# A block-recurrent cross-attention with a three-way maxout FFN: a head in a new order, with the second slice of batch 0 ahead of the third slice of G

## The chip, the core and the metric

The kernel runs on one core of a Trainium2 chip. The metric is device time in microseconds, lower is better; the time of a kernel is the median of several runs. A core has a matrix engine (TensorE, PE in the profile, which also shows its weight loads as PEld), a vector engine (VectorE, DVE), a scalar engine (ScalarE, ACT), a general engine (GpSimd, POOL) and a sync engine (SyncE, SP). DMA is issued from the queues of SP, ACT and POOL. PE writes only into PSUM, and ACT and DVE carry results out of it.

## The reference

Sizes: batch B = 8, heads H = 8, sequence S = 512, states Ns = 32 for each head, width D = 64; d_model = 512, d_ff = 768. Inputs and output are float32.

```python
scores  = x @ state^T / sqrt(64);  a  = softmax(scores, over states)
xread   = a @ state
scores2 = state @ x^T / sqrt(64);  a2 = softmax(scores2, over tokens)
sread   = a2 @ x
y   = concat([xread, sread], axis=2)          # rows of a batch: 512 tokens, then 32 states
y   = y.transpose(0, 2, 1, 3).reshape(8 * 544, 512)
h   = maximum(maximum(y @ w1, y @ w2), y @ w3)
out = h @ w_out
```

## The kernel before

Per batch the kernel never forms `xread`. It builds G = (block-diagonal states) @ W for the three matrices at once (`g_slice` and `g_run`, L363 of `g_mm`), so that the first layer is `pw = G^T aT`, with `aT` the transposed attention weights. One slice of the first layer is 128 of the 768 columns of d_ff for one batch: `layer1(b, m)` issues 6 matmuls into three PSUM banks, one for each matrix (L416). Three instructions make the maximum of the three: ACT copies the first bank to SBUF (`max_first`, L431), and DVE takes the maximum with the second bank (`max_second`, L436) and with the third (`max_third`, L440), which writes `ht`. The second layer is `layer2(b, j)`: 6 matmuls into one bank (L447), which ACT or DVE copies out (L454).

Ahead of that, for each batch: `x` is loaded and transposed (`xT`; by PE for batches 0 and 1, by a transposing DMA on SP's queue for the others), the scores are 16 small matmuls (L262), ACT exponentiates them (L269), DVE sums and inverts (L276, L278), POOL (or DVE) multiplies (L284), and the weights are transposed to `aT` (by PE at L295 for batches 0 and 1, by DMA afterwards). The states' own read is `sread` (L327).

The states come in four loads of two batches each, `load_st(k, q)` for batches 2k and 2k+1 on queue q (L152, tiles `stf0` to `stf3`). `states_cast` casts them (L217), `states_turn` transposes them on PE (L222, tile `pt`) and `states_place` copies them into the block-diagonal tile `bd` (L228). Everything of batches 2 and 3 that uses `bd` stands behind the load of `stf1`.

W1, W2 and W3 arrive in pieces by `load_w(m0, m1, i)`: columns 128*m0 to 128*m1 of matrix i (0, 1, 2) on POOL's queue (L179). G's slice m of batches 0 and 1 needs these columns of all three matrices.

The order is written out by hand: strings of short words (`FIRST`, `EACH` once for each batch, `LAST`) are walked by `perform`, and each word calls one function, whose instructions go to their engines in that order. So every engine runs its own instructions in the order of the words, and waits where a semaphore says so. The words that matter here: `lst` load states, `stc`/`stt`/`stp` cast, turn and place them, `lw` load a piece of W, `lxg` load half of a batch of x (four of its eight heads), `g`/`gc` a slice of G and its copies out, `l1` a slice of layer 1, `m0`/`ma`/`mb` its three maximum instructions, `l2`/`l2c` layer 2 and its copy, `busy` one filler matmul of 512 columns on a zero tile (`keep_busy`, L211), whose result nobody reads. A letter behind a word names the engine or queue (A for ACT, D for DVE, P for POOL, S for SP). `BANKS` gives the PSUM bank of each one-bank tile in order of use (four banks), `PAIRS` that of each two-bank tile. The words of one batch in `EACH` make PE run, for batch b and the one before it: 24 + 6 + 6 layer-1 matmuls, 24 layer-2 matmuls, the scores, G and `sread`.

Behind all this stands a branch that redoes the softmax with a maximum subtracted if a sum left a safe range; it is not taken with these inputs.

Of the kernel before, what the change touches and what calls it, by code (L numbers as in the profile page):

```python
# [17 lines left out]
FIRST = """  # L18
    lst 0 A; lxu 0 0 S; zero; clr 0; clr 1; clr 2; clr 3; warm; lxg 0 1; busy 1; xones 1; ident; busy 1;
    lxg 1 0; busy 1; busy 1; stc 0 D; busy 1; busy 1; busy 1; busy 1; busy 1; lxg 1 1; stt 0; busy 2;  # L20
    cxu 0 0 D; xt 0 0; stp 0 A; busy 1; xt 0 1; busy 1; xtc 0 0 D; lw 0 2 1; lw 0 2 2; xtc 0 1 D;
    busy 1; sc 0 0; busy 1; lw 0 1 0; busy 1; sc 0 1; lw 1 3 0; ex 0 0; busy 1; busy 1; xt 1 0; sum 0 0;
    lw 2 3 1; busy 1; ex 0 1; sum 0 1; xt 1 1; busy 1; xtc 1 0 AD; busy 1; lw 2 3 2; busy 1; xtc 1 1 A;
    busy 1; wt 0 0 P; wt 0 1 P; xones 0; sc 1 0; ex 1 0; busy 1; sc 1 1; at 0 0; atc 0 0 A; sr 0;
    busy 1; sum 1 0; lw 3 4 0; at 0 1; lst 1 A; lw 3 6 2; lw 3 6 1; ex 1 1; wt 1 0 D; g 0 0; gc 0 0 D;
    busy 1; sum 1 1; g 1 0; sr 1; atc 0 1 A; lw 4 6 0; wt 1 1 P; at 1 0; srs 0; g 1 1; g 0 1; stc 1 P;
    l1 0 0; gc 1 1 D; gc 1 0 A; g 1 2; g 0 2; atc 1 0 A; busy 1; gc 0 1 A; m0 0 0; at 1 1; lxg 2 1;
    srs 1; ma 0 0; l1 0 1; lxg 2 0; gc 0 2 A; l1 0 2; atc 1 1 D; l1 1 0; m0 0 1; m0 0 2; lwo; m0 1 0;
    gc 1 2 A; mb 0 0; xtd 2; l1 1 1; g 0 3; m0 1 1; lst 3 S; lst 2 A; ma 0 1; gc 0 3 A; g 1 3; pad 2;
    stt 1; gc 1 3 A; mb 0 1; ma 0 2; mb 0 2; ma 1 0; mb 1 0; l1 1 2; ma 1 1; g 0 5; m0 1 2; ones; g 0 4;  # L30
    mb 1 1; stp 1 DA; l1 0 3; gc 0 4 A; ma 1 2; g 1 4; gr 2 1792 2304; gc 0 5 D; m0 0 3; mb 1 2; l1 1 3;
    l1 0 5; gc 1 4 A; gr 2 0 512; g 1 5; m0 1 3; ma 0 3; mb 0 3; ma 1 3; l1 1 4; grc 2 1792 2304 A;
    mb 1 3; m0 0 5; gr 2 1280 1792; stc 2 P; lxg 3 1; gr 2 512 1024; ma 0 5; l1 0 4; stt 2; sc 2 -;
    gc 1 5 A; m0 1 4; grc 2 0 512 D; mb 0 5; lxg 3 0; ma 1 4; grc 2 1280 1792 AD; m0 0 4; ma 0 4;
    mb 0 4; mb 1 4; xtd 3; l2 0 3; l2 0 1; ex 2 -; l1 1 5; stp 2 A; l2c 0 3 D; stc 3 P; l2 0 2; sum 2 -;
    l2c 0 1 D; stt 3; l2 0 0; m0 1 5; ma 1 5; l2c 0 2 A; grc 2 512 1024 D; wt 2 - P; sr 2; mb 1 5;
    srs 2; gr 2 1024 1280; l2c 0 0 D; so 0 0 2 P; lx 4; so 0 2 4 P; stp 3 A; grc 2 1024 1280 A; atd 2;
"""
EACH = """
    pad 1; gr 1 1792 2304; gr 1 0 512; grc 1 1792 2304 AD; l2 -1 0; l2 -1 1; l1 0 0; grc 1 0 512 D;  # L40
    l2c -1 0 A; m0 0 0; sc 1 -; l2 -1 3; gr 1 1024 1280; ex 1 -; xtd 2; gr 1 1280 1792; l2c -1 1 D;
    ma 0 0; gr 1 512 1024; mb 0 0; sr 1; grc 1 1024 1280 A; l1 0 1; l1 0 2; sum 1 -; l1 0 3; srs 1;
    l1 0 5; l2c -1 3 A; m0 0 1; m0 0 2; ma 0 1; mb 0 1; ma 0 2; m0 0 3; mb 0 2; srt -2; ma 0 3;
    wt 1 - P; m0 0 5; mb 0 3; l2 -1 2; grc 1 1280 1792 A; grc 1 512 1024 A; ma 0 5; mb 0 5; l2c -1 2 D;
    l1 0 4; so -1 2 4 P; m0 0 4; ma 0 4; lx 3; mb 0 4; atd 1; ap -2 A; so -1 0 2 P;
"""
LAST = """
    srt 6; l1 7 0; srt 7; l2 6 0; l1 7 2; m0 7 0; l1 7 3; l1 7 4; ap 7 D; m0 7 2; srt 5; ap 6 A; ma 7 0;
    m0 7 3; mb 7 0; ap 5 A; l2c 6 0 D; ma 7 2; l2 6 1; l1s 0; l2 6 2; m0 7 4; mb 7 2; l1 7 1; l2c 6 1 A;
    ma 7 3; m0 s 0; l2c 6 2 A; l1s 2; l1 7 5; ma 7 4; mb 7 4; look; ma s 0; m0 7 1; m0 s 2; mb s 0;  # L50
    so 6 2 3 S; m0 7 5; mb 7 3; l1s 1; ma 7 1; mb 7 1; ma s 2; mb s 2; ma 7 5; m0 s 1; ma s 1; l1s 5;
    so 6 0 1 S; mb 7 5; l2p 7 2 384 512; l1s 3; m0 s 5; ma s 5; mb s 1; m0 s 3; mb s 5;
    l2pc 7 2 384 512 A; l2p 7 0 384 512; l2p 7 3 256 512; sop 7 2 384 512 P; ma s 3; l2p 7 2 128 384;
    mb s 3; l2p 7 0 0 128; l2pc 7 0 0 128 A; l2pc 7 3 256 512 D; l2p 7 1 0 128; l2p 7 3 0 256;
    l2pc 7 0 384 512 D; flag; l2pc 7 1 0 128 A; l2pc 7 2 128 384 A; l1s 4; m0 s 4; l2 6 3;
    sop 7 0 0 128 P; ma s 4; sop 7 0 384 512 P; mb s 4; l2p s 0 256 512; so 6 1 2 P; l2 s 1;
    sop 7 3 256 512 A; l2c 6 3 D; l2p 7 2 0 128; sop 7 1 0 128 S; l2p s 0 0 256; so 6 3 4 A;
    l2pc 7 3 0 256 D; l2pc s 0 256 512 D; sop s 0 256 512 A; l2pc 7 2 0 128 A; l2p 7 1 128 384;
    sop 7 2 0 128 A; l2p 7 0 256 384; l2p 7 1 384 512; l2pc s 0 0 256 A; l2p 7 0 128 256;
    l2pc 7 1 128 384 A; l2c s 1 D; sop 7 3 0 256 S; sop 7 2 128 384 P; l2pc 7 0 256 384 D;  # L60
    sop 7 1 128 384 A; l2pc 7 1 384 512 D; sop 7 1 384 512 A; l2pc 7 0 128 256 D; sop 7 0 128 256 A;
    sos 1 S; sop s 0 0 256 S; sop 7 0 256 384 S; hold; vl;
"""

BANKS = """
# [3 lines left out]
"""  # L69
PAIRS = """  # L70
    0101100101 1010010010 1010101010 1010101010 10
# [4 lines left out]
def kernel(  # L76
# [21 lines left out]
    J = 4  # L98
# [19 lines left out]
    st = [data.tile([128, 4, 2, D], BF16, name=f"st{k}") for k in range(B // 2)]  # L118
# [15 lines left out]
    xT, e, a, aT, G, ht, osb, xp = {}, {}, {}, {}, {}, {}, {}, {}  # L134
    open_ps = {}

    def new(d, b, shape, name, bufs=2):
        d[b] = work.tile(shape, BF16, tag=name, bufs=bufs, name=name)


    homes = {n: iter("".join(t.split())) for n, t in (("b", BANKS), ("w", PAIRS))}
# [28 lines left out]
    def load_x_uncast(b, g, q):  # L170
        o = work.tile([128, J, d_model], F32, tag="osb", bufs=3, name="osb")
        x_f[b, g] = o.rearrange("p j f -> p (j f)")[:, 0:HS * J * D].rearrange("p (s jd) -> p s jd", s=HS)
        queue[q].dma_start(out=x_f[b, g], in_=x_heads(b, g))
# [42 lines left out]
    def states_cast(k, c):  # L216
        copier[c](out=st[k], in_=st_f[k].unsqueeze(2).to_broadcast((128, 4, 2, D)))  # L217

    def states_turn(k):
        p = open_ps["st", k] = bank([128, 4, 128], BF16, "pt")  # L220
        for t in range(4):
            nc.tensor.transpose(p[:, t, :], st[k][:, t].rearrange("p c d -> p (c d)"), ident)  # L222

# [7 lines left out]
    def x_turn(b, g):  # L231
        if g == 0:
            new(xT, b, [128, H, 2, 128], "xT", bufs=3)
# [7 lines left out]
    def x_turned(b, g, c):  # L241
        p, w = open_ps.pop(("x", b, g)), HS // len(c)
# [4 lines left out]
    def x_turn_dma(b):  # L247
        new(xT, b, [128, H, 2, 128], "xT", bufs=3)
        nc.sync.dma_start_transpose(out=xT[b].rearrange("p h j t -> p (h j) t"), in_=x_sb[b][:, 0:XW])

# [3 lines left out]
    def scores(b, g=None):  # L254
        if not g:
            new(e, b, [128, J, 2, HS, Ns], "e")
# [11 lines left out]
    def exps(b, g=None):  # L268
        nc.scalar.activation(out=parity(e[b], g), in_=open_ps.pop(("s", b, g)), func=AF.Exp, scale=scale)  # L269
# [10 lines left out]
    def weights(b, g, c):  # L280
        if not g:
            new(a, b, [128, J, 2, HS, Ns], "a")
# [7 lines left out]
    def a_turn(b, g):  # L290
        if g == 0:
            new(aT, b, [128, J, 2, 128], "aT", bufs=3)
# [4 lines left out]
    def a_turned(b, g, c):  # L297
        copier[c](out=aT[b][:, :, g, :], in_=open_ps.pop(("a", b, g)))

    def a_turn_dma(b):  # L300
        new(aT, b, [128, J, 2, 128], "aT", bufs=3)
# [4 lines left out]
    def pad(b):  # L306
        xp[b] = work.tile([128, HS, J, 2 * D + 2], BF16, tag="xp", name="xp")
# [7 lines left out]
    def sread(b):  # L315
        w = D + 1 if b in xp else 2 * D
        p = open_ps["r", b] = bank([128, 2, w], F32, "psr")
        for j in range(J):
            for g in range(2):
                for s in range(HS):  # L320
                    if b in xp:
                        both = xp[b][:, s, j, g * D:g * D + D + 1]
                    else:
# [4 lines left out]
                        p[32 * s:32 * s + 32, g], e[b][:, j, g, s, :], both,  # L328
# [38 lines left out]
    def new_g(b):  # L367
        if b not in G:
            new(G, b, [128, 2, 3, d_ff], "G", bufs=3)


    def g_slice(b, m):
        new_g(b)
# [4 lines left out]
    def g_sliced(b, m, c):  # L378
        p = open_ps.pop(("g", b, m))
# [5 lines left out]
    def g_run(b, c0, c1):  # L385
        new_g(b)
        n = c1 - c0
        if n > 256:
# [9 lines left out]
    def g_ran(b, c0, c1, c):  # L398
        p, ps = open_ps.pop(("g", b, c0))
# [10 lines left out]
    def maxout(b, m, n, lhs, rhs, nk, by_k=False):  # L410
        if m == 0 and b not in ht:
# [132 lines left out]
    def perform(plan, base=0):  # L544
        for op in plan.replace("\n", " ").split(";"):
# [5 lines left out]
            if batches and args[0] != "s":  # L551
                args[0] += base
                if args[0] >= B:
                    continue
# [123 lines left out]
```

## Time and profile before

| | us |
|---|---|
| median of 3 runs | 153.05 |
| lowest and highest | 152.54, 153.25 |
| span of the profiled execution, first to last instruction | 151.4 |
| the median less that span | 1.6 |
| PE, DVE, ACT, POOL busy | 146.4, 118.9, 82.8, 57.0 |

The time of the profiled execution itself is not given apart from its span; what lies around the span is taken as 1.6 us, from the median of the runs. In the profile a line such as L416 is a line of the kernel before; `out<-in` names tiles with buffer numbers left out; times count from the first instruction. The granted TensorE clock of this execution is 1.000 in the view by cores.

### The profile page before, as it was taken

Reading aid. Unit: us, or ns where it says so; the run is one execution under the profiler, and the core shown is the slowest. Engines: PE = TensorE matmul, PEld = TensorE weight load, DVE = VectorE, ACT = ScalarE, POOL = GpSimd, SP = SyncE. Lnnn points to the kernel's source line nnn. Section 1 sums busy time; section 2 is a strip of 40 time slices with the busy share of each in tenths; the row PEclk is TensorE's granted clock in tenths of the full one; section 3 lists DMA queues with packets and bytes.
Section 4 is the critical chain, followed back from the end, with each engine's and each line's share of the span. In section 5 each row is a group of like instructions: output and inputs, shape, how many; then the busy total and the mean of one; then the engine's idle time right before and its main releaser. Section 6 shows DMA issues by size and latency. Waiting matters only on the chain.

```text
span 151.4 us, 3635 instructions
## 1 busy us (share of the span) xinstructions
PE 146.4 (97%) x1431; PEld 73.8 (49%) x1431; DVE 118.9 (79%) x204; ACT 82.8 (55%) x143; POOL 57.0 (38%) x79
## 2 busy tenths in 40 slices
PE   6999799999999999999999999999999999999992
PEld 2566343335445443544354435443544446679771
DVE  6477698999977898879987988798879887675353
ACT  3368558976364665466646664666466653331220
POOL 6979650561528505540554046414331200001500
PEclk9999999999999999999999999999999999999999
DMA  3999999979737979999589749974503250300455
GB/s 115 211 189 195 207 198 195 151 149 139 139 74 167 230 59 265 129 223 132 155 124 230 144 130 140 232 122 141 218 0 78 68 226 4 122 18 17 175 180 196
DMA packets 39108, 22.29 MB, mean 147 GB/s; under 512 B 23072, under 2 KB 36896, under 8 KB 39088
## 3 DMA queue, kind: packets, MB, share of 16 engines
q0 software_dynamic: 15872, 13.96, 48.7%
q1 hardware_dynamic: 21776, 6.82, 23.4%
q10 hardware_dynamic: 1440, 1.25, 2.7%
q8 instruction: 12, 0.20, 0.5%
q14 instruction: 8, 0.07, 0.2%
HBM read 15.20 MB, written 8.91 MB: 159 GB/s over the span
## 4 chain that ended last, share of the span: by engine, by line
PE 86%; DMA 6%; POOL 4%; issue 1%; DVE 1%; POOLq 0%
PE pw L416 46%; PE po L447 25%; DMA w<-in_moe_w_dram 6%; PE pg L363 5%; PE po L462 4%; POOL w L179 2%; PE ps L262 2%; PE psr L327 2%; POOL x L168 1%; PE pgh L363 1%; PE pt L222 1%; DVE held L522 0%; PE idle L520 0%; PE idle L211 0%; DVE osb L466 0%
## 5 line engine op out<-in xcount | busy, mean ns | idle before, releaser
L416 PE MATMUL pw<-aT,G 128*128 128x512 bf16 x288 | 66.8, 379 | 0.0
L431 ACT CAST t<-pw 128x512 bf16<-128x512 f32 (+1 forms) x54 | 30.4, 564 | 28.9 <-PE pw L416 27.2
L416 PEld LDWEIGHTS <-G 128*128 128x128 bf16 x288 | 27.2, 98 | 33.2 <-issue 1.9
L436 DVE TENSOR_TENSOR t<-t,pw 128x512 bf16<-128x512 bf16 (+1 forms) x54 | 35.4, 655 | 9.5 <-ACT t L431 7.4
L447 PE MATMUL po<-wout,ht 128*128 128x512 bf16 x168 | 39.9, 379 | 0.0
L440 DVE TENSOR_TENSOR ht<-t,pw 128x512 bf16<-128x512 bf16 x48 | 32.9, 687 | 4.3
L447 PEld LDWEIGHTS <-ht 128*128 128x128 bf16 x168 | 15.3, 98 | 19.0 <-issue 1.7
L284 POOL TENSOR_TENSOR a<-e,rden 128x1024 bf16<-128x1024 bf16 (+1 forms) x9 | 14.5, 1620 | 24.1 <-ACT osb L454 11.1
L477 POOL DMA_DIRECT2D out_dram<-osb x13 | 7.4, 572 | 30.5 <-ACT t L431 27.5
L403 ACT CAST G<-pg 128x1024 bf16<-128x1024 f32 (+1 forms) x17 | 14.3, 875 | 1.3 <-PE pg L363 1.3
L311 POOL COPY xp<-x 128x1024 bf16<-128x1024 bf16 x12 | 12.3, 1062 | 5.5 <-DMA x<-in_x_dram 5.5
L454 DVE COPY osb<-po 128x512 f32<-128x512 f32 x16 | 10.9, 684 | 2.4 <-PE po L447 2.3
L276 DVE TENSOR_REDUCE seen<-e 128x32 f32<-128x1024 bf16 (+1 forms) x10 | 10.0, 999 | 3.6 <-ACT e L269 3.6
L403 DVE CAST G<-pg 128x1024 bf16<-128x1024 f32 (+1 forms) x13 | 12.2, 972 | 0.7 <-ACT G L403 0.7
L454 ACT COPY osb<-po 128x512 f32<-128x512 f32 x13 | 7.7, 593 | 8.9 <-PE po L447 8.9
L269 ACT ACTIVATE e<-ps 128x1024 bf16<-128x1024 f32 (+1 forms) x10 | 8.5, 854 | 6.6 <-PE ps L262 6.4
L363 PE MATMUL pg<-w,bd 64*32 64x512 bf16 (+1 forms) x288 | 10.8, 362 | 0.9 <-DMA w<-in_moe_w_dram 0.9
L211 PE MATMUL idle<-zero 128*128 128x512 bf16 x27 | 10.0, 477 | 1.3 <-DVE zero L187 1.3
L472 POOL DMA_DIRECT2D out_dram<-osb x4 | 2.2, 544 | 19.4 <-ACT osb L466 19.4
L381 ACT CAST G<-pg 128x768 bf16<-128x768 f32 x9 | 7.1, 801 | 3.3 <-PE pg L363 3.1
L416 PE MATMUL pw<-atp,w 128*128 128x256 bf16 x72 | 8.7, 272 | 0.0
L416 PEld LDWEIGHTS <-w 128*128 128x128 bf16 x72 | 6.9, 98 | 1.5
(70 smaller groups left out, 116.0 us busy)
## 6 DMA issues: line engine op xcount, KB each, us to landing
out_dram<-osb POOLq DMA_DIRECT2D x12, 512.0 KB, 3.5
x<-in_x_dram POOLq DMA_DIRECT2D x4, 512.0 KB, 7.3
x<-in_x_dram POOLq DMA_DIRECT2D x7, 256.0 KB, 5.5
w<-in_moe_w_dram POOLq DMA_DIRECT2D x4, 256.0 KB, 7.5
w<-in_moe_w_dram POOLq DMA_DIRECT2D x2, 384.0 KB, 7.9
wout<-in_moe_w_out_dram POOLq DMA_DIRECT2D x1, 768.0 KB, 11.6
out_dram<-osb SPq DMA_DIRECT2D x3, 256.0 KB, 2.4
osb<-in_x_dram SPq DMA_DIRECT2D x1, 512.0 KB, 4.0
```

The source lines that it names most:

```text
L211: nc.tensor.matmul(p, zero[:, 0:128], zero, start=True, stop=True)
L276: nc.vector.reduce_sum(out=den, in_=parity(e[b], g), axis=AX.X)
L284: times[c](out=parity(a[b], g).rearrange("p j g s n -> p j (g s) n"), in0=parity(e[b], g).rearrange("p j g s n -> p j (g s) n"), in1=rdens ...
L311: nc.gpsimd.tensor_copy(out=xp[b][:, :, :, g * (D + 1):g * (D + 1) + D], in_=v[:, g])
L363: nc.tensor.matmul(p(s, g), bd(b, 2 * s + g)[64 * g:64 * g + 64, g, :], f(w_sb[64 * g:64 * g + 64, s]), start=True, stop=True, tile_positi ...
L403: copier[c[g]](out=v[:, g:h], in_=p[:, g:h, 0:c1 - c0])
L416: nc.tensor.matmul(pw[i][:, 0:n], lhs(i, k), rhs(k), start=(k == 0), stop=(k == nk - 1))
L431: nc.scalar.copy(out=t0s[b, m][:, 0:n], in_=open_ps["l", b, m][0][:, 0:n])
L436: nc.vector.tensor_max(t1s[b, m][:, 0:n], t0s.pop((b, m))[:, 0:n], open_ps["l", b, m][1][:, 0:n])
L440: nc.vector.tensor_max(ht[b][:, m, :], t1s.pop((b, m))[:, 0:n], open_ps.pop(("l", b, m))[2][:, 0:n])
L447: nc.tensor.matmul(p, ht[b][:, m, j * 128:(j + 1) * 128], wout_sb[:, m, :], start=(m == 0), stop=(m == NM - 1))
L454: copier[c[i]](out=o[:, j, i * w:i * w + w], in_=p[:, i * w:i * w + w])
```

## The change

The three strings become one flat string, `PLAN`, in which the head (everything up to the first steps of batch 3) stands in another order; from batch 4 on the blocks name, on PE, the same steps in the same order as before, written out for each batch, and the end of the program has the same steps on PE. `BANKS` and `PAIRS` are written anew to fit. A table `PLACES` names the buffer of each work tile, where before a pool rotated two, three or four of them; the buffer is taken when the tile is first written instead of when it is first mentioned. The cast states (`st`) lie in two buffers instead of four. The program before has 27 filler matmuls ahead of the last one that closes the program; the changed one has 17.

```diff
-FIRST = """
-    lst 0 A; lxu 0 0 S; zero; clr 0; clr 1; clr 2; clr 3; warm; lxg 0 1; busy 1; xones 1; ident; busy 1;
...
-    l1 0 0; gc 1 1 D; gc 1 0 A; g 1 2; g 0 2; atc 1 0 A; busy 1; gc 0 1 A; m0 0 0; at 1 1; lxg 2 1;
...
+PLAN = """
+    lst 0 A; lxu 0 0 S; lxg 0 1; zero; ident; lxg 1 0; xones 0; xones 1; lxg 1 1; lw 0 1 0; lw 0 2 2; lw 0 2 1;
...
+    sr 1; atc 0 1 A; at 1 0; g 0 1; gc 1 0 A; atc 1 0 A; srs 1; gc 0 1 D; g 1 1; l1 0 0; m0 0 0; ma 0 0;
+    gc 1 1 AD; lst 1 A; wt 1 1 P; lw 3 6 2; at 1 1; atc 1 1 A; l1 0 1; m0 0 1; mb 0 0; ma 0 1; mb 0 1; g 0 2;
...
 BANKS = """
-    0123012301 2302013012 0130120203 2012313031 3210130213 2012302130 1231021301 2310210230 1320312312
+    0332000013 2131011300 2310132011 2031023021 3201230123 0213021032 0130213021 3012310201 0213201203 1201321031
...
+    def turned(j):
+        return j % 2 * 2 + j // 2
...
     def exps(b, g=None):
-        nc.scalar.activation(out=parity(e[b], g), in_=open_ps.pop(("s", b, g)), func=AF.Exp, scale=scale)
+        new(e, b, [128, J, 2, HS, Ns], "e")
+        nc.scalar.activation(
+            out=parity(e[b], g).rearrange("p (c i) g s n -> p i c (g s n)", i=2),
+            in_=open_ps.pop(("s", b, g)).rearrange("p (i c) g s n -> p i c (g s n)", i=2),
+            func=AF.Exp, scale=scale)
...
+    def tokens(b, j):
+        k = j if b == "s" else turned(j)
+        return slice(k * 128, k * 128 + 128)
+
     def layer2(b, j):
...
-            nc.tensor.matmul(p, ht[b][:, m, j * 128:(j + 1) * 128], wout_sb[:, m, :],
+            nc.tensor.matmul(p, ht[b][:, m, tokens(b, j)], wout_sb[:, m, :],
```

The four token blocks of a batch now lie in another order in `e`, `a` and `aT` (0, 2, 1, 3): ACT writes the exponentials that way in one instruction of as many elements, and `sread` and layer 2 pick the blocks accordingly. Functions for a transposed score path are added and not called.

Three places of the new order, for the engines on which they lie. The first is ACT at the first slices of layer 1. `G_334` and `G_350` are G of batches 0 and 1 before (`G_326` and `G_388` now), `pg` is the PSUM tile of one of their slices, `aT_396` (`aT_390`) is `aT` of batch 1, `t0` is the copy of the first bank of a layer-1 slice, `stf1` the states of batches 2 and 3. Before:

```order
L381 CAST G_350<-pg_351 128x6x128
L298 COPY aT_396<-pat_397 128x4x128
L381 CAST G_334<-pg_414 128x6x128
L431 CAST t0_458<-pw0_425 128x512
L381 CAST G_334<-pg_445 128x6x128
L431 CAST t0_502<-pw0_471 128x512
L431 CAST t0_504<-pw0_482 128x512
```

and now:

```order
L444 CAST G_388<-pg_331 128x6x128
L362 COPY aT_390<-pat_374 128x4x128
L492 CAST t0_414<-pw0_405 128x512
L444 CAST G_388<-pg_396 128x3x128
L190 DMA stf1_75<-in_state_dram 128x256
L362 COPY aT_390<-pat_423 128x4x128
L492 CAST t0_438<-pw0_429 128x512
L444 CAST G_326<-pg_445 128x6x128
```

Between the copies of the first and the second layer-1 slice of batch 0 (`t0_458` and `t0_502`, now `t0_414` and `t0_438`) stood the copy of G's third slice of batch 0 (`G_334<-pg_445`); it now stands behind both (`G_326<-pg_445`). ACT's copy of G's second slice of batch 0 (`G_334<-pg_414`) is gone from it (DVE does it), half of that of batch 1 has come, the second half of `aT` of batch 1 too, and the load of `stf1`, which stood six rows above `t0_458`, follows the first slice now.

The second place is POOL's queue of loads, from the second matrix pieces on. Here `w` pieces of 128 columns have the size 128x4x128, `a` is the product at L284, and `x2` is batch 2. Before:

```order
L179 DMA w_94<-in_moe_w3_dram 128x4x128
L284 TENSOR_TENSOR a_251<-e_180,rden_221 128x4x128
L284 TENSOR_TENSOR a_251<-e_180,rden_228 128x4x128
L198 MEMSET x0_86 128x64
L179 DMA w_94<-in_moe_w1_dram 128x4x128
L179 DMA w_94<-in_moe_w3_dram 128x4x384
L179 DMA w_94<-in_moe_w2_dram 128x4x384
L179 DMA w_94<-in_moe_w1_dram 128x4x256
L284 TENSOR_TENSOR a_332<-e_255,rden_348 128x4x128
L217 CAST st1_79<-stf1_75 128x512
L168 DMA x2_88<-in_x_dram 128x4x256 x2
```

and now:

```order
L217 DMA w_90<-in_moe_w2_dram 128x4x128
L217 DMA w_90<-in_moe_w2_dram 128x4x384
L349 TENSOR_TENSOR a_233<-e_194,rden_200 128x4x128
L349 TENSOR_TENSOR a_233<-e_194,rden_226 128x4x128
L217 DMA w_90<-in_moe_w1_dram 128x4x128
L349 TENSOR_TENSOR a_324<-e_260,rden_266 128x4x128
L349 TENSOR_TENSOR a_324<-e_260,rden_322 128x4x128
L217 DMA w_90<-in_moe_w3_dram 128x4x384
L206 DMA x2_84<-in_x_dram 128x4x256
L217 DMA w_90<-in_moe_w1_dram 128x4x256
L206 DMA x2_84<-in_x_dram 128x4x256
```

One 384-column piece of W is issued ahead of the products of batch 0, both products of batch 1 are POOL's (DVE did one), one half of `x2` goes ahead of the last piece of W (256 columns of W1), and the cast of `stf1`, which stood ahead of both halves, is behind these rows. Higher up in the same queue the first piece of W1 is issued ahead of those of W2 and W3 instead of behind them.

The third place is SP's queue at its start. `osb` is the first half of batch 0's x, loaded as float32 into an output buffer, and `stf3` holds the states of batches 6 and 7. Before:

```order
L173 DMA osb_105<-in_x_dram 128x4x256
L249 DMA_TRANSPOSE xT_511<-x2_88 128x16x128
L152 DMA stf3_77<-in_state_dram 128x256
L249 DMA_TRANSPOSE xT_763<-x3_89 128x16x128
L302 DMA_TRANSPOSE aT_880<-a_823 128x8x128
```

and now:

```order
L211 DMA osb_101<-in_x_dram 128x4x256
L190 DMA stf3_77<-in_state_dram 128x256
L291 DMA_TRANSPOSE xT_610<-x2_84 128x16x128
L291 DMA_TRANSPOSE xT_823<-x3_85 128x16x128
L366 DMA_TRANSPOSE aT_834<-a_817 128x8x128
```

The load of `stf3` stood behind the transpose of batch 2, which waits for all of `x2`; it now goes out as the second transfer of the program.

More of the change, by code (lines that the diff above doesn't have):

```diff
@@ L38 @@
[L38 to L45, printed above, removed]
@@ L117 @@
     st_f = [data.tile([128, 4, D], F32, name=f"stf{k}") for k in range(B // 2)]
-    st = [data.tile([128, 4, 2, D], BF16, name=f"st{k}") for k in range(B // 2)]
+    st = {}
     bds = [data.tile([128, 2, H, 2, Ns], BF16, name=f"bd{k}") for k in range(B // 2)]
@@ L548, in perform @@
             name, *args = op.split()
-            f, batches = table[name]
-            args = [value(t) for t in args]
[L551 to L554, printed above, removed]
-            f(*args)
-    perform(FIRST)
-    for b in range(2, B - 1):
-        perform(EACH, b)
-    perform(LAST)
+            table[name](*(value(t) for t in args))
+    perform(PLAN)
     def scores_below_max(b):
@@ L607 @@
     homes["b"], homes["w"] = cycle("0123"), cycle("01")
+    places = {}
     with tc.If(bad != 0, label="again"):
         for b in range(B):
-            for d in (xT, e, a, aT, G, ht, osb, xp):
+            for d in (xT, eT, e, a, aT, G, ht, osb, xp):
                 d.pop(b, None)
```

236 lines of the change are left out of this document (151 added, 85 removed), and 2 rows, old and new, of the table BANKS.

## The prediction

> **What bounds the kernel now.** I read the page's first parts, then the chain of waits in order of time, then busy times by stretch. The page first: PE is busy for all but 5 us of the span, and nothing else comes near.
>
> ```profile
> span 151.4 us, 3635 instructions
> PE 146.4 (97%) x1431; PEld 73.8 (49%) x1431; DVE 118.9 (79%) x204; ACT 82.8 (55%) x143; POOL 57.0 (38%) x79
> ```
>
> The share is a mean over stages, so here are four stretches (span; then busy us and count of each engine, clock, share and rate of DMA):
>
> ```profile
> core 0: us, PE busy (x) PEld busy (x) DVE busy (x) ACT busy (x) POOL busy (x), PEclk, DMA share, GB/s
> 16.00:18.00 2.00, 1.14 (x13) 0.39 (x19) 1.84 (x5) 1.01 (x2) 1.14 (x2) 1.00 1.37 200
> 18.00:20.00 2.00, 2.00 (x27) 0.97 (x26) 0.99 (x2) 1.36 (x2) 2.00 (x4) 1.00 1.33 202
> 20.00:36.00 16.00, 16.00 (x161) 6.57 (x159) 14.96 (x24) 11.57 (x19) 5.84 (x10) 1.00 1.20 168
> ...
> 50.15:65.40 15.25, 15.25 (x157) 6.80 (x160) 12.90 (x21) 9.00 (x17) 6.05 (x7) 1.00 0.98 172
> ```
>
> From 20 us on PE has no idle time. In the batches' steady stretch (15.25 us each) DVE has 2.35 us to spare, but from 20 to 36 it is busy 14.96 of 16.00, 93.5%: that stage has two bounds side by side. PE's last hole lies at 16 to 18, and the chain of waits says what it is (start, duration, what):
>
> ```profile
> 8.17 9.70 DMA w<-in_moe_w_dram
> 17.91 0.52 PE pg L363 x16
> 18.43 0.32 PE idle L211
> 18.75 0.22 PE pat L295 x4
> 18.97 5.20 PE pw L416 x24
> ...
> 24.62 0.33 PE pt L222 x4
> ...
> 26.35 0.45 PE pg L363 x16
> ...
> 38.57 1.29 PE pw L416 x6
> ...
> 42.68 0.38 PE psr L327 x30
> ...
> 47.72 0.47 PE ps L262 x16
> ...
> 50.15 0.38 PE psr L327 x27
> 50.53 5.30 PE pw L416 x24
> ```
>
> A piece of W that was issued at 8.17 lands at 17.86, PE computes G's third slice from it, runs one filler, and from 18.97 the chain is PE alone but for its last pieces. A layer-1 slice is 6 matmuls in 1.29 us. The timeline gives what stood before the hole:
>
> ```profile
> 15.58 1.47 PE L416 MATMUL pw<-aT,G 128*128 128x512 bf16 x6
> 16.41 0.60 ACT L431 CAST t<-pw 128x512 bf16<-128x512 f32 x1
> 15.93 0.95 DVE L381 CAST G<-pg 128x768 bf16<-128x768 f32 x1
> 19.01 0.42 DVE L298 COPY aT<-pat 128x512 bf16<-128x512 bf16 x1 [1.14 <-PE pat L295]
> ```
>
> The first slice begins at 15.58, so its successor could have begun at 15.58 + 1.29 = 16.87.
>
> **The change part by part.** *After the head nothing changes on PE.* From `sread` of batch 3 (50.15 above) to the end PE's steps stand in the same order, with the same operands' sizes. What matters is how much earlier or later PE reaches that point.
>
> *Second slice ahead of G's third.* PE now has a transpose of `aT` and a layer-1 slice to do (0.22 + 1.29) where it stood still: the hole 17.91 - 16.87 = 1.04 goes. The filler behind it goes too, 0.32. Together -1.36. The third slice's W lands near 17.9, and PE asks for it at about 16.87 + 0.22 + 1.29 = 18.4, so that wait is hidden by 0.5. The second slice of G, which the moved slice reads, is now a cast of DVE's (0.95 in the row above) instead of one of ACT's: done by 16.9 if it starts at 15.93 as DVE's cast did, and needed at 17.1.
>
> *States 6 and 7 first.* 128 KB more go out beside the first half of x. The trace has no such case alone. The issue rows and the states' landing times bound it:
>
> ```profile
> osb<-in_x_dram SPq DMA_DIRECT2D x1, 512.0 KB, 4.0
> ...
> DMA to landing us min/median/max: 2.8/4.5/8.1
> ```
>
> 512 KB took 4.0 us beside the first states' 2.8 for 128 KB: (4.0 - 2.8) / 3 = 0.4 for each further 128 KB. At 200 GB/s (the 16-to-18 stretch) it is 0.66; if it fits between the first transfers it is nothing. I take 0.40, the nearest in time, and count it in full, as everything behind it in the queues (x, then W) sets PE's start: +0.40. PE's lead at 19 us is then 0.96.
>
> *The half of x ahead of W's last piece.* That piece was issued at 14.4 and took:
>
> ```profile
> L179 POOL DMA_DIRECT2D w<-in_moe_w_dram x1: 770/770/770, 14.4 to 14.4; - x1
> DMA to landing us min/median/max: 9.1/9.1/9.1
> ```
>
> It landed at 23.5; 256 KB ahead of it at 200 GB/s make 1.3, the states 0.4: 25.2. PE used it at 26.35, now 26.35 - 0.96 = 25.4. Hidden by 0.2, so priced at nothing; with that cover gone it costs what it is late, some tenths.
>
> *DVE in the second stage.* PE's lead lasts only if DVE keeps up. A slice costs DVE two maxima:
>
> ```profile
> L436 DVE TENSOR_TENSOR t<-t,pw 128x512 bf16<-128x512 bf16 x11 | 7.5, 682 | 0.3 <-ACT t L431 0.2
> L440 DVE TENSOR_TENSOR ht<-t,pw 128x512 bf16<-128x512 bf16 x10 | 6.8, 685 | 0.7
> ```
>
> That is 1.37 us against PE's 1.29, in only four one-bank PSUM tiles, so PE cannot run ahead by much more than it does. For DVE: its idle 1.14 at 19.01 gets the moved slice's maxima, one `aT` copy (0.42) leaves it, and two casts of G are split with ACT, which has 4.4 us free from 20 to 36. Against: it was at 93.5% already, and a stage 0.96 shorter with about 0.9 less to do is at the same share. Ends: nothing given back, or all 0.96. I take half, since row and tally point to opposite ends: +0.48.
>
> *The rest* goes together at nothing: the exponentials in four strides (same 1024 elements, ACT has room), explicit buffers, POOL's later padding of batch 2 (needed by that batch's `sread`, 42.68 in the chain).
>
> Sum: -1.04 - 0.32 + 0.40 + 0.48 = -0.48 on the span of 151.4, so 150.9; with the 1.6 around it and against the median of 153.05: **152.6**.
>
> **The rivals.** *(1) The states of batches 2 and 3 come late: slower.* Their load moves on ACT behind the first slice's copy. In the trace:
>
> ```profile
> 12.26 0.35 ACTq L152 DMA_DIRECT2D stf<-in_state_dram  x1
> 17.71 0.61 POOL L217 CAST st<-stf 128x512 bf16<-128x512 f32 x1 [0.86 <-DMA stf<-in_state_dram]
> ...
> 23.33 0.34 ACTq L152 DMA_DIRECT2D stf<-in_state_dram  x1
> ...
> 26.38 4.75 SPq L249 DMA_TRANSPOSE xT<-x  x1
> ```
>
> The first of these landed 5.4 us after its issue, the second, which met a transposing DMA, 8.1 (the maximum above). Now the issue comes at 16.41 + 0.60 + about 0.4 for half a cast of G, 17.4, and PE's transpose of these states, at 24.62 before, at 23.66. Less the cast, 0.61, they must land by 23.05: in 5.65 us. With 5.4 nothing happens; with 8.1 PE stands 2.45, nothing is left to give back to DVE, and the sum is -1.36 + 0.40 + 2.45 = +1.5: 154.5. Queued behind the waiting transpose are all of PE, and on ACT and DVE the copies of `bd`. For 5.4: at 17 to 23 us the queues are full of W as they were at 12 to 17, and no transposing DMA runs. Against: a margin of a quarter of a microsecond. Slower by over 0.5% from 7.4 us on.
>
> *(2) PE's clock opens later: slower.* The fillers at the start show it:
>
> ```profile
> 1.27 4.02 PE L211 MATMUL idle<-zero 128*128 128x512 bf16 x9 [1.27 <-DVE zero L187]
> 5.51 0.91 PE L211 MATMUL idle<-zero 128*128 128x512 bf16 x2
> 6.70 0.38 PE L211 MATMUL idle<-zero 128*128 128x512 bf16 x1
> ```
>
> Nine fillers back to back take 4.02 us, 0.43 each; at 6.70 one is over in 0.38, end modelled. So the fast rate came between. Now seven stand there, several on the same PSUM bank in a row, which must wait for each other, and 17 in all instead of 27. If the fast rate came as late again, at about 11, the transposes and scores of two batches would run at half rate: eight times 4 transposes (0.22 each four in the chain) and twice 16 score matmuls (0.47), 2.7 us by their fast times, and fillers and waits cover about half: +1.35, so 153.9. The Trainium skill, "TensorE: Matmul & The Clock Gate", Part 1, says that the clock is raised after about 3.4 us of sustained busy time in a window that runs freely; by that a filler less could cost one more window, an estimate of 3.4 us at half rate. The traced switch, some 5 us after the first filler, allows it. Against: seven fillers of 0.43 still fill 3 of the 4 us.
>
> *(3) The whole lead stays: faster.* DVE's relief suffices and the states' load hides: between -0.96 and -1.36, say 151.9. For it: ACT's free time. Against: the 93.5%.
>
> *(4) The change doesn't do what it says.* The moved slice waits for DVE's cast of G's second slice, only 0.2 early; a DVE queue 1 us late puts the hole back, and with the states' 0.40 the time is 153.3.
>
> **How the numbers follow.** A measurement of this kernel can tell about 0.5%, 0.77 us, from no change. Forecast 0.40, a seventh of it beyond 0.77 faster; (1) 0.15, two thirds of it slower, the rest within; (2) 0.10, slower; (3) 0.20, faster; (4) 0.12, within; something unseen 0.03, slower. Faster 0.06 + 0.20 = 0.26; slower 0.10 + 0.10 + 0.03 = 0.23, and within 0.51. The forecast's own range, from the ends of its terms: all of -1.36 kept (151.7) to all given back and 0.66 for the states, with W's last piece a few tenths late (153.4). With the rivals, 151.7 to 154.3 holds 8 in 10.
>
> **What would show it.** Right: no wait for W at 16 to 19, two slices of layer 1 ahead of G's third, `sread` of batch 3 about 0.5 us earlier than 50.15, 15.25 us for each batch after it, and between 24 and 36 short waits of PE for DVE's maxima, about half a microsecond in all. Wrong: a wait of `pt` at 23 to 26 for the states (rival 1), fillers at 0.43 after 7 us (rival 2), or a shift that arises after 50 us, which nothing here explains.

## The result: slower by 2.5%

| | us, median | lowest to highest | runs |
|---|---|---|---|
| before | 152.74 | 152.25 to 153.25 | 8 |
| changed | 156.76 | 155.71 to 165.4 | 8 |

The ratio is 1.0245, 95% interval 1.0214 to 1.0276. The forecast was 152.6, with 151.7 to 154.3 as the range: the change was to give 0.4 us and cost 4.0.

Two of the eight runs of the changed kernel took 164 to 165 us (single runs of other kernels, the one before among them, were as long) and lie outside the ratio, and the profile that came with them is of one of these, so the lines below are of a second profile of the same kernel (experiment e0, 157.32 us, span 155.4).

### The profile page after: what moved, and what is told of

Read it like the earlier page. It is cut to its first block, busy times and chain, and to the rows that moved or that the text cites. A ratio compares the mean times of both kernels' runs of the same rounds, so it can differ in the third digit from the quotient of the medians.

```text
span 163.6 us, 3607 instructions
## 1 busy us (share of the span) xinstructions
PE 148.8 (91%) x1407; PEld 74.4 (45%) x1421; DVE 116.8 (71%) x202; ACT 85.3 (52%) x146; POOL 57.7 (35%) x80
## 4 chain that ended last, share of the span: by engine, by line
PE 54%; DMA 5%; DVE 1%; issue 1%
PE pw L477 30%; PE po L514 15%; DMA aT<-a 5%; PE po L532 4%; PE pg L427 2%; PE ps L305 1%; PE psr L391 1%; PE pgh L427 1%; DVE held L593 0%; PE idle L591 0%; DVE osb L537 0%; PE pst L575 0%
## 5 line engine op out<-in xcount | busy, mean ns | idle before, releaser
L477 PE MATMUL pw<-aT,G 128*128 128x512 bf16 x288 | 68.6, 384 | 6.5 <-DMA aT<-a 6.2
L349 POOL TENSOR_TENSOR a<-e,rden 128x1024 bf16<-128x1024 bf16 (+1 forms) x10 | 15.6, 1566 | 39.3 <-ACT G L469 11.4
L466 ACT CAST G<-pg 128x1024 bf16<-128x1024 f32 (+1 forms) x19 | 16.8, 912 | 2.2 <-PE pg L427 2.2
L526 ACT COPY osb<-po 128x512 f32<-128x512 f32 x16 | 9.5, 591 | 9.1 <-PE po L514 9.1
L526 DVE COPY osb<-po 128x512 f32<-128x512 f32 x13 | 8.9, 687 | 3.2 <-PE po L514 3.2
L466 DVE CAST G<-pg 128x512 bf16<-128x512 f32 (+1 forms) x10 | 9.2, 950 | 2.3 <-ACT G L466 2.3
L249 PE MATMUL idle<-zero 128*128 128x512 bf16 x16 | 7.7, 542 | 1.5 <-DVE zero L225 1.3
L217 POOL DMA_DIRECT2D w<-in_moe_w_dram x10 | 7.6, 782 | 0.0
```

Source lines behind the costliest of these rows:

```text
L349: times[c](out=parity(a[b], g).rearrange("p j g s n -> p j (g s) n"), in0=parity(e[b], g).rearrange("p j g s n -> p j (g s) n"), in1=rdens ...
L466: copier[c[g]](out=v[:, g:h], in_=p[:, g:h, 0:c1 - c0])
L477: nc.tensor.matmul(pw[i][:, 0:n], lhs(i, k), rhs(k), start=(k == 0), stop=(k == nk - 1))
L526: copier[c[i]](out=o[:, j, i * w:i * w + w], in_=p[:, i * w:i * w + w])
```

## The profile after

The page's first parts, and the busy times by stretch (span; busy us and count of each engine, clock, share and rate of DMA), where the prediction showed those of before:

```profile
span 155.4 us, 3607 instructions
...
PE 146.1 (94%) x1407; PEld 73.4 (47%) x1421; DVE 116.7 (75%) x202; ACT 85.3 (55%) x146; POOL 57.7 (37%) x80
```

```profile
core 0: us, PE busy (x) PEld busy (x) DVE busy (x) ACT busy (x) POOL busy (x), PEclk, DMA share, GB/s
16.00:18.00 2.00, 2.00 (x28) 1.02 (x13) 1.87 (x5) 1.38 (x4) 2.00 (x3) 1.00 1.46 185
...
20.00:36.00 16.00, 15.72 (x142) 6.12 (x142) 14.01 (x23) 12.41 (x21) 5.52 (x10) 1.00 1.22 187
```

PE's busy time is about what it was (146.1 against 146.4) and the span is 4.0 us longer: this is waiting, not work. The hole at 16 to 18 is gone (2.00 busy of 2.00, 1.14 in the profile of before), and from 20 to 36 PE now has 0.28 us idle. The chain of waits in order of time:

```profile
17.85 1.33 PE pw L477 x6
19.18 0.45 PE pg L427 x16
19.63 4.00 PE pw L477 x18
...
26.19 0.69 issue
26.88 0.70 DVE t L497
27.62 0.59 PE pw L477 x2
...
42.89 0.48 DVE osb L526
43.38 4.69 DMA aT<-a
48.12 1.47 PE pw L477 x6
```

The second slice and G's third follow one another without a wait for W, as forecast. Two things are new: VectorE stands in the chain at 27, and batch 2's transposing DMA, issued at 43.38, at 43 to 48; PE waits for its landing. In the kernel before neither was in it. `sread` of batch 3 (start, duration), now and then before:

```profile
51.48 0.45 PE L391 MATMUL psr<-xp,e 128*32 128x65 bf16 x32
```

```profile
50.08 0.45 PE L327 MATMUL psr<-xp,e 128*32 128x65 bf16 x32
```

The prediction wanted it half a microsecond earlier; it is 1.40 late. From there on a batch takes 15.25 us, as before. The end, by the timeline:

```profile
149.96 0.38 PE L591 MATMUL idle<-zero 128*128 128x512 bf16 x1 [0.38 <-DVE osb L537]
150.38 0.69 DVE L593 CAST held<-idle 128x512 bf16<-128x512 f32 x1 [0.47 <-PE idle L591]
```

Before, the same two rows read

```profile
148.57 0.38 PE L520 MATMUL idle<-zero 128*128 128x512 bf16 x1 [0.38 <-DVE osb L466]
148.99 0.69 DVE L522 CAST held<-idle 128x512 bf16<-128x512 f32 x1 [0.47 <-PE idle L520]
```

This is the reading that splits the loss. The last work is 1.39 us late (150.38 against 148.99), as late as `sread` of batch 3 was, but from its start to the end of the span pass 5.0 us (155.4 - 150.4) where it was 2.4. **More than half of the loss lies behind the last work.** The page counts no branch as busy, so the rows for it are the trace's own records of VectorE's sequencer (us from the span's start; "behind" is the first instruction that ran after the branch):

```
kernel                       flag load  branch   behind   branch to behind
before (316 instructions)      149.00   149.62   150.19        0.57
changed, e0 (318)              150.39   151.39   154.26        2.87
```

On the other engines 0.2 to 0.5 us pass from the branch to the next instruction; their last waits end with VectorE's (at 154.70 in e0).

## The experiments

"Instructions" of VectorE below are those of the main block up to and with the branch over the fall-back code: 316 before, 318 in the changed kernel (four more semaphore waits, two operations fewer).

**e0, e1, e2, e3: the first suspects.** Again the changed kernel; then two edits of the order, alone and together:

```diff
 e1, e3:
- atd 2; pad 3; gr 3 1792 2304;
+ atd 2; gr 3 1792 2304;
- so 0 2 4 P; l2 1 1;
+ so 0 2 4 P; pad 3; l2 1 1;
 e2, e3:
- busy 1; busy 1; warm;
+ busy 1; busy 1; busy 1; busy 1; warm;
```

(e2 and e3 also give the fillers PSUM banks in turn.)

> The changed kernel once more, for a second profile: the first showed PE standing 5.9 us before layer 1 of batch 3 (aT landed 8.5 us after its issue) and the clock opening at 9.1 us instead of 6.1. Queue theory (the load of batch 4's x is issued about 1 us later behind the padding of batch 3 on POOL, and SP's transposes queue up behind it): again x of batch 4 lands after 55 us, aT of batch 3 is issued at about 60 beside the output store and the load of batch 5, and PE waits for it, between 2 and 9 us. Clock theory alone: no such wait, and the whole loss of about 1 us lies before 16 us.

> The changed kernel with batch 3's padding put back behind batch 4's load on POOL, nothing else. Queue theory: the load goes out near 43.5 to 45 instead of 46.1, lands near 53, aT of batch 3 is in time, no wait of PE for it, and the time falls from 156.8 to about 153.7 (the head's loss of 1 us stays). Clock theory alone: within 0.3 us of 156.

> The changed kernel with nine fillers in three banks at the start instead of seven in banks 0, 3, 3, 2, 0, 0, 0. Clock theory: the fast rate is reached by about 6 us instead of 9, the first layer-1 slice begins 0.5 us earlier (15.8 instead of 16.3); time 0.5 us lower than the changed kernel if the wait for aT stays, and more if 0.5 us is enough to end it. If the clock's window runs freely and has nothing to do with the fillers: no change beyond the runs' spread.

> Both edits together. If queue and clock are the two causes: within 0.3 us of the kernel before (152.7), or up to 0.5 faster, since PE's lead at 20 us is then about 0.9. If the exchange of the slices itself costs time in the stage from 24 to 50 us, still 0.5 to 1 us slower than before.

Measured: 157.32; 156.75 (ratio 1.0243, 1.0211 to 1.0274); 156.6 and 156.7 in two runs of e2, 163 in the two others; 156.25 (1.023, 1.0188 to 1.0272), against 152.87. Each edit alone gives nothing, both together 0.5 us at most, and the intervals do not tell that from nothing. Neither the queue theory nor the clock theory accounts for the loss. But in e3 the last work is as early as before, and the span is not:

```profile
148.68 0.38 PE L591 MATMUL idle<-zero 128*128 128x512 bf16 x1 [0.38 <-DVE osb L537]
149.09 0.69 DVE L593 CAST held<-idle 128x512 bf16<-128x512 f32 x1 [0.47 <-PE idle L591]
```

149.09 against 148.99, span 154.4 against 151.4. The tail was the thing to test.

**e4 and e5: only the tail, in the kernel before.** One clearing of a state buffer at the start (e4), or two (e5), are each written as two half ones, which does nothing but lengthen VectorE's stream by one or two instructions:

```diff
- nc.vector.memset(bds[k], 0.0)
+ for j in ([0, 1] if k in (2, 3) else [slice(0, 2)]):   # e4: k in (3,)
+     nc.vector.memset(bds[k][:, j], 0.0)
```

> The kernel before, with one of the four clearings of a state buffer on VectorE written as two half ones: VectorE has 317 instructions ahead of the closing branch instead of 316 (the changed kernel has 318); nothing else moves. In the profiles of the changed kernels VectorE's last work ended as early as before (149.1 + 0.69 us in the run with both edits, 149.0 + 0.69 before) but the instruction behind its branch began 2.8 to 3.3 us after the branch, and 0.57 us before. Theory P (the place of VectorE's branch in its instruction stream decides it): no bound here whether one more is enough: either as before, 152.9, or 155.5 to 156. Theory T (the closing wait comes from what the DMA engines do in the changed order, not from the place of the branch): 152.9, the instruction behind the branch 0.5 to 0.6 us after it.

> The same with two clearings halved: VectorE has 318 instructions ahead of its branch, as many as the changed kernel. Theory P: 155.5 to 156 (152.9 + 2.6 to 3.1), an interval of the ratio wholly above 1.015, the instruction behind the branch 2.8 to 3.3 us after it, and a ninth or further 8 KB instruction fetch. Theory T: 152.9, ratio 1.000.

Measured: e4 152.91 (ratio 1.0006, 0.9979 to 1.0034), e5 155.63 (1.0182, 1.0139 to 1.0225), against 152.77. One more instruction costs nothing, two cost 2.86 us. (The lower end of e5's interval is a little under the 1.015 that was expected.) The page's rows on instruction fetches in e4:

```profile
q8 instruction: 12, 0.20, 0.5%
q14 instruction: 8, 0.07, 0.2%
```

and in e5:

```profile
q8 instruction: 12, 0.20, 0.5%
q14 instruction: 9, 0.07, 0.2%
```

(queue, packets, MB, share). One 8 KB packet more, as in all kernels with 318. The sequencer's records:

```
kernel                       flag load  branch   behind   branch to behind
e4, before + 1 (317)           148.63   149.25   149.81        0.56
e5, before + 2 (318)           148.69   149.69   152.88        3.19
```

The branch itself comes 0.38 us later after the load (1.00 against 0.62), and what is behind it 2.6 us later: together 3.0, about the measured difference. The theory of the transfers falls, that of the branch's place stands. Over all profiles with 318 instructions the wait is 2.3 to 2.7 us beyond the usual 0.57.

Why this place is a bad one is not shown. The Trainium skill, "Runtime: NRT & Kernel Launch", section "Instruction fetch mechanics", says that a taken branch whose target isn't in the window of fetched pages forces a fetch before execution goes on. The trace agrees that the branch's place decides, but shows no such fetch: the two 8 KB packets inside e5's wait (150.38 and 150.48) come in e4 too (150.41 and 150.56), are over by 150.94, and the next, the ninth in the page's count, begins at 153.48, after VectorE has gone on at 152.88.

**e6 and e7: the other way.** The changed kernel, and e3's, with two clearings moved from VectorE to GpSimd, so that VectorE has 316 again:

```diff
- nc.vector.memset(bds[k], 0.0)
+ (nc.gpsimd if k in (1, 3) else nc.vector).memset(bds[k], 0.0)
```

(and the tokens `clr 1; clr 3;` moved in front of `stc 1 P`).

> The changed kernel with the clearing of two state buffers (those of batches 2/3 and 6/7) done on GpSimd behind W_out's load instead of VectorE at the start: VectorE has 316 instructions ahead of its branch, as the kernel before. Theory P: 156.8 less 2.6 to 3.1 = 153.7 to 154.2, the instruction behind the branch 0.6 us after it; what is left over before (about 1 us) is the order's own. Theory T: 156.5 to 157.

> The same with the two edits of the run with both (pad of batch 3 behind the output store, two more fillers at the start): TensorE's useful work there stood within 0.2 us of before from 48 us on. Theory P: 156.25 less 2.6 to 3.1 = 153.2 to 153.6, ratio 1.001 to 1.006. Theory T: 156.2.

Measured: e7 153.56 (ratio 1.0069, 1.004 to 1.0097), 2.69 less than e3, the branch to what is behind it 0.57. e6 scattered (154.38 to 162.32, ratio 1.0181, 1.0099 to 1.0263) and says little of the time, though its trace has 0.57 there too. So 2.7 to 2.9 us of the 4.0 are the branch's place, 0.5 at most the fillers and the pad, and 0.8 is left that belongs to the order. (e10 and e14 below have 317 instructions, and 0.56 there.)

**e9: what the exchange is worth in the new order.** An edit of e7's kernel:

```diff
- l1 0 1; m0 0 1; mb 0 0; ma 0 1; mb 0 1; g 0 2; g 1 2; l1 1 0;
+ g 0 2; g 1 2; l1 0 1; m0 0 1; mb 0 0; ma 0 1; mb 0 1; l1 1 0;
```

> The kernel of the run with both edits and 316 instructions, with the change's first part undone: batch 0's second slice of layer 1 behind G's third slices instead of ahead of them. The prediction took 0.83 us for that part. In the kernel that is edited TensorE's lead in useful work over before was 1.5 us at 24, 0.4 at 40 and -0.2 from 48 us on. Theory K (the part's gain is kept to the end): 154.2 to 154.5. Theory G (it is given back by 40 us to evictions that come no earlier, and the rest at the wait for batch 2's a): 153.4 to 153.8.

Measured: 154.67 (1.012, 1.0095 to 1.0145), 1.77 over the 152.90 of before, where e7 is 0.79 over 152.77: the gain, 1.0 us, is there and is kept. Some 0.4 of it is a longer wait for batch 2's `a` (1.0 against 0.6 in e7). The timeline of e9:

```profile
17.10 0.55 DVE L444 CAST G<-pg 128x384 bf16<-128x384 f32 x1
...
17.70 0.52 PE L427 MATMUL pg<-w,bd 64*32 64x384 bf16 x16 [0.78 <-DVE G L444]
```

With the exchange undone PE waits again, but not for W: for VectorE's half of the second slice's cast, which frees the pair of banks that G's third slice writes.

**e11 and e13: the exchange in the old order.** The kernel before with the exchange alone, and then with batch 1's first slice behind it, as in the changed kernel:

```diff
 e11:
- l1 0 0; gc 1 1 D; gc 1 0 A; g 1 2; g 0 2; atc 1 0 A;
+ l1 0 0; gc 1 1 D; gc 1 0 A; atc 1 0 A;
- l1 0 1; lxg 2 0;
+ l1 0 1; g 1 2; g 0 2; lxg 2 0;
 e13, beside this:
- gc 0 2 A; l1 0 2; atc 1 1 D; l1 1 0; m0 0 1; m0 0 2; lwo; m0 1 0;
+ m0 0 1; gc 0 2 A; atc 1 1 D; l1 1 0; l1 0 2; m0 1 0; lwo; m0 0 2;
- ma 0 2; mb 0 2; ma 1 0; mb 1 0;
+ ma 1 0; mb 1 0; ma 0 2; mb 0 2;
```

> The kernel before with only the first part of the change: batch 0's second slice of layer 1 (with the transpose of batch 1's a in front of it) ahead of both third slices of G; all else, the 316 instructions of VectorE among it, as before. Undoing that part in the run with both edits cost 1.0 us (154.67 against 153.56). If the part is worth that in the old order too: 151.7 to 152.2, ratio 0.992 to 0.996. If VectorE gives it back in the stage behind (the prediction's 0.48 of 1.36, the filler still there) : 152.2 to 152.5. If the old order had it hidden elsewhere: 152.8 to 153.

> The run with the exchange alone in the old order (154.29 us) showed where its gain went: behind G's third slice of batch 0 stood the layer-1 slice that reads it, and TensorE waited 1.09 us (19.48 to 20.57) for ScalarE's cast; ScalarE had the second slice's first eviction queued behind that cast, so VectorE stood 2.04 us. Here batch 1's first slice stands between, as in the changed kernel, and that eviction ahead of the cast. If the exchange's worth hangs on what follows it: no wait at 16 to 21 us above 0.3, 151.7 to 152.4, ratio below 0.998. If the old order behind it has no use for the lead: 152.6 to 153.2.

Measured: e11 154.29 (1.0104, 1.0087 to 1.0121), slower by 1.5 us. In its timeline the hole has only moved:

```profile
19.13 0.52 PE L363 MATMUL pg<-w,bd 64*32 64x384 bf16 x16
19.72 0.80 ACT L381 CAST G<-pg 128x768 bf16<-128x768 f32 x1 [2.52 <-PE pg L363]
...
20.57 1.80 PE L416 MATMUL pw<-aT,G 128*128 128x512 bf16 x6 [0.93 <-ACT G L381]
21.04 0.69 DVE L436 TENSOR_TENSOR t<-t,pw 128x512 bf16<-128x512 bf16 x1 [2.04 <-ACT t L431]
```

Right behind G's third slice stands the layer-1 slice that reads it, so PE waits out the whole cast, and the moved slice's first eviction is queued behind that cast, so VectorE stands 2.04. With other work between (e13) PE goes on:

```profile
18.88 0.52 PE L363 MATMUL pg<-w,bd 64*32 64x384 bf16 x16
...
19.33 2.50 PE L416 MATMUL pw<-aT,G 128*128 128x512 bf16 x10
```

and the time is 152.98 (1.0011, 0.9992 to 1.003): no difference that can be told, not the 0.3 to 1 us that was expected. The traces suggest why. The piece of W for which PE stood in the prediction's profile is issued at 8.17 in all kernels of the old order. It landed at 17.86 there, but at 15.80 in e11, 15.96 in e13, and, with the exchange not made, at 15.93 in e4 and 16.32 in e5. In e4 the stretch reads

```profile
16.00:18.00 2.00, 2.00 (x31) 0.76 (x24) 1.93 (x7) 1.47 (x3) 1.73 (x3) 1.00 1.32 194
```

and e4's last work begins 0.37 us earlier than in the prediction's profile (148.62 against 148.99). Of the three profiles of the order before only the prediction's has the hole of 1.04 us; what delayed W in it, and how often that happens, is open.

**e10, e12, e14 and e8: the wait for batch 2's `a`.** In e7's timeline:

```profile
45.71 0.63 PE L305 MATMUL ps<-bd,xT 128*128 128x64 bf16 x16
...
46.98 1.25 PE L477 MATMUL pw<-aT,G 128*128 128x512 bf16 x5 [0.64 <-DMA aT<-a]
```

Three edits of e7's kernel try to have `a` earlier (e12 and e14 with a third clearing moved to GpSimd):

```diff
 e10:
- sc 2 -; l1 1 5; m0 1 5; ma 1 5; ex 2 -; l2 0 1; l2 0 2; sum 2 -; l2c 0 1 A;
+ sc 2 -; l1 1 5; ex 2 -; m0 1 5; l2 0 1; l2 0 2; sum 2 -; ma 1 5; l2c 0 1 A;
 e12:
- l2c 0 3 A; sc 2 -; l1 1 5; m0 1 5; ma 1 5; ex 2 -; l2 0 1;
+ l2c 0 3 D; sc 2 -; l1 1 5; ex 2 -; m0 1 5; ma 1 5; l2 0 1;
 e14: as e10, with l2c 0 3 D
```

and e8, on e7 too, writes ten fillers as four 128-column matmuls each, to move PE's instruction fetch:

```diff
- busy 1;
+ part 1;
...
+ for c in range(4 * n):
+     v = slice(c % 4 * 128, c % 4 * 128 + 128)
+     nc.tensor.matmul(p[:, v], zero[:, 0:128], zero[:, v], start=True, stop=True)
```

> The kernel of the run with both edits and 316 instructions on VectorE (153.56 us), with ten of the fillers at the start written as four 128-column matmuls each instead of one of 512 columns: the same streaming time, 60 more instructions in TensorE's stream, so that its 16 KB instruction fetches fall some 2.3 us (60 instructions at 26 a us) earlier in the work: the one at 44.46 us at about 42, before the transposing DMA of batch 2's a (issued 42.44) moves its packets. There that DMA landed 4.49 us after its issue and TensorE stood 0.64 us for it; in the kernel before, where the fetch (43.99) came behind its last packet, 2.71 us. Theory F (the fetch in the middle of the DMA delays it): landing 2.6 to 3.2 us after issue, no wait of TensorE at 47, 152.8 to 153.1. Theory S (the output store and the load of x that GpSimd issues 0.8 to 1.4 us behind it delay it): 4 us or more, 153.4 to 153.8.

> The kernel of the run with both edits and 316 instructions, with batch 2's exponentials on ScalarE ahead of the eviction of batch 1's last slice (and the sum on VectorE ahead of that slice's first maximum): a of batch 2 is ready about 0.5 us earlier, so its transposing DMA is issued at about 41.9 instead of 42.44. Theory W (TensorE's wait at 47 us for that DMA is carried to the end): 153.0 to 153.2. Rival (the late eviction, or a landing that is not earlier, takes its place): 153.5 to 153.8.

> The kernel of the run with both edits (153.56 us), with batch 2's exponentials ahead of the eviction of batch 1's last slice once more, and with the eviction of layer 2's third token block of batch 0 on VectorE instead of ScalarE in front of them, so that ScalarE begins them as soon as the scores are there; a third clearing goes to GpSimd, VectorE has 316 instructions. In the run with the exponentials early TensorE stood 1.2 us at 38.6 for a PSUM bank that the late eviction held, in place of 0.64 at 47. Theory W (with that eviction 0.6 us earlier the bank is free in time, and the transposing DMA of batch 2's a, issued at 41.5 or earlier, lands ahead of TensorE's 16 KB fetch at 44.5): landing 2.7 us after issue, no wait above 0.3 us at 38 and 47, 152.8 to 153.1. Rival (one of the two waits stays): 153.4 to 154.2.

> As the last run with the exponentials early (155.06 us, where VectorE took the maximum of batch 1's last slice ahead of the sum, the transposing DMA of batch 2's a was issued at 42.33, no earlier than without the edit, and TensorE's 16 KB fetch came 2.2 us behind it: landing 5.4 us after issue, a wait of 1.85), with the sum ahead of that maximum. Issue at 41 or earlier and landing 2.7 us later, ahead of the fetch: no wait at 47; the wait at 38.6 for the PSUM bank 0.6 instead of 1.2: 153.2 to 153.6. If the landing follows the fetch alone however early the issue: 4 us or more, 154 or more.

Measured: e10 154.24 (1.0093), e12 155.06 (1.0175), e14 153.80 (1.0079, 1.0052 to 1.0106), none better than e7. In e10 and e14 the wait at 47 is gone, and another has come, by e10's timeline:

```profile
37.62 0.59 ACT L492 CAST t<-pw 128x512 bf16<-128x512 f32 x1
...
39.30 0.63 DVE L497 TENSOR_TENSOR t<-t,pw 128x512 bf16<-128x512 bf16 x1
...
39.98 1.24 PE L514 MATMUL po<-wout,ht 128*128 128x512 bf16 x5 [1.01 <-DVE t L497]
```

Layer 2 needs a PSUM bank that the last slice's maximum still holds: the rival of e10's expectation (the same wait is 0.7 in e14). e12 is worse than either of its theories: its DMA was issued at 42.33, no earlier, and PE waited 1.7 for it. e8 failed as an experiment: the fetch came at 44.85, not at 42, and its six runs took 152.89, 154.33 and 158 to 162.

What lengthens the landing? The records of that DMA in the profiles that tell it apart (batch 3's where said; us; "fetch" is PE's 16 KB instruction fetch):

```
kernel              issued   fetch after issue   landed after issue
before               41.60        2.39                2.71
e4                   41.13        2.42                2.71
e13                  40.98        2.48                2.71
e10                  41.47        3.13                2.70
e14                  41.52        3.17                2.70
changed, e0          43.38        2.46                4.69
e7                   42.44        2.02                4.49
e12                  42.33        2.16                5.43
e9                   43.33        1.29                4.86
e3, batch 3          54.94        2.23                4.26
before, batch 3      57.55        none                2.80
```

Where the fetch falls 1.3 to 2.2 us behind the issue, the landing takes 4.2 to 5.4 us (the other profiles give 4.2 to 4.7 for 1.8 to 2.0); later than that, 2.7, with one exception (e0). In the kernel before this DMA's own packets moved from 1.2 to 2.3 us behind its issue (42.78 to 43.88), so a fetch in the first band falls among them and a later one behind them. The rival of e8's expectation, GpSimd's store and load of x, is not needed: in e3 no packet of GpSimd's queue moved before batch 3's landing, which took 4.26 all the same. (In the kernel before 53 did, but in the last 0.6 us.) But no run moved the fetch alone, so the fetch as the cause is supported and not shown.

## Why the prediction was wrong, point by point

- **"After the head nothing changes on PE."** True of PE, and the step that failed: the argument ended with PE's last work and put the sum on the whole span of 151.4, so it took the 2.4 us from the last work to the span's end at no change, without a reason. They became 5.0. (The 1.6 around the span hardly matter: 1.9 in e0.) The order that moves casts between engines also adds four semaphore waits to VectorE and takes two operations off, and these two instructions more put its closing branch at a place where the next instruction comes 2.87 us behind it instead of 0.57 (the price in whole runs: 2.86 in e5, 2.69 from e3 to e7). Why that place is slow stays open. No rival had it; the prediction's "a shift that arises after 50 us, which nothing here explains" is what came.
- **The second slice ahead (-1.36).** The second step that failed. Its 1.04 was read off one execution; in e4 and e5, in the same order, W lands 1.5 to 1.9 us earlier and the hole is not there, so by them only the filler's 0.32 was to be won. In the old order the exchange gives nothing (e13) or costs 1.5 (e11). That undoing it in the new order costs 1.0 (e9) is no proof of the term: there it is the cast that frees the banks which makes PE wait. A step's worth depends on what then stands behind it.
- **States 6 and 7 first (+0.40).** Not shown. The second half of batch 0's x landed at 7.28 in e0 and 6.91 before, 0.37, but that is within the scatter: 6.80 in e7, which has the same load in front, and 6.57 in e4. It was not run by itself.
- **W's last piece (0).** Right: predicted landing 25.2, landed 24.93, and PE began on it at 25.69 without a wait.
- **VectorE gives back 0.48.** Right in kind, mis-sized: the gaps between PE's layer-1 matmuls beyond their usual spacing sum from 24 to 34 us to 1.06 us in e7 (0.32, 0.29, 0.14, 0.14, 0.17) and 0.11 before, 0.95 instead of 0.48. A row of it in e7 shows the form:

```profile
25.22 0.69 DVE L271 COPY bd<-pt 64x512 bf16<-64x512 bf16 x1 [0.40 <-ACT bd L271]
...
25.94 0.69 DVE L497 TENSOR_TENSOR t<-t,pw 128x512 bf16<-128x512 bf16 x1
25.97 1.31 PE L477 MATMUL pw<-aT,G 128*128 128x512 bf16 x4 [0.15 <-DVE bd L271]
```

  The states' placing is now shared by ScalarE and VectorE, one half waits for the other, and the maxima behind it are late. Half was a choice between two ends, and the upper one came; the tally of busy time that spoke for less does not see such an order.
- **Batch 2's transposing DMA.** Not in the prediction: its issue 1.8 us later (43.38 against 41.60) and its landing in 4.69 instead of 2.71 made the wait of 0.6 to 0.8 at 47. Counted by the columns of its matmuls, PE in e7 is 1.5 us ahead of the prediction's profile at 24 us, 0.55 at 46 and 0.25 behind from 48 on: VectorE takes 0.95 and this wait 0.8. That e7 would win back its 0.79 without the wait is not shown, as e10 and e14 put another in its place.
- **Rival (1), the states late: did not come.** Issued 16.81, landed 21.76, 4.95 us, and cast at once; the margin held.
- **Rival (2), the clock.** In part. By the clock's records the fast rate came at 8.65 us in e0 and at 6.13 before. With the seven fillers of the changed kernel it came at 7.3 to 9.1 in four profiles, with nine at 4.2 to 7.1 in seven, and in the old order at 5.8 to 7.2 in five, so part of the difference is scatter. PE's first layer-1 slice began at 16.16 in e0 and 15.22 in e7 (15.58 before), but in the time fillers and pad together gave at most 0.5 us (156.76 to 156.25), against the 1.35 it priced.
- **Rival (3), the whole lead stays: did not come.** VectorE gave back 0.95 of it.
- **Rival (4), the hole back through VectorE's cast.** Not in the changed kernel. e9 shows its like, 0.78 us, but there it is G's third slice that waits for the cast, and not the moved slice.

In sum, by the steps between the medians: 0.5 (fillers and pad, 156.76 to 156.25, not clear of noise) + 2.7 (branch, to 153.56) + 0.8 (order, to 152.77) = 4.0, as measured. In the traces of e0 and before: 1.4 up to `sread` of batch 3 and 2.6 behind the last work.

## What to carry to other kernels

Compare the span's end with the end of the last work before explaining anything in between: a loss there is not in the order of the work. Where a kernel ends in a branch, count the instructions of each engine before and after a change, waits too, and try one or two more or fewer: here 317 on VectorE were fast and 318 slow, and no run says where the limit lies in another program. Before pricing a hole, see in a second profile of the same order whether it is there. Read a hole's releaser on every engine that frees or fills it; closing the one in sight pays only if what stands behind the moved work does not wait for the same thing.

## What the hardware showed that was not expected

- Two instructions more in front of VectorE's branch cost 2.86 us, one costs nothing (e5, e4).
- The same transfer of W, issued at 8.17 in five profiles of the old order, landed anywhere from 15.80 to 17.86 us.
- A transposing DMA that usually lands 2.7 us after its issue took 4.2 to 5.4 where PE's instruction fetch came 1.3 to 2.2 us behind it (once 2.5), and 8.3 to 8.9 in three executions: in e8's profile (span 159.4 us) batch 2's was issued at 44.13 and landed at 52.98, beside a store and a load of 512 KB issued at 44.94 and 45.55. PE stood 5.0 us for it, and its granted clock then fell to half for 3.4 us; in e6's profile, after a landing of 8.33 us for batch 3's and a wait of 4.5, for 6.8 us.
